# Two attention + FFN layers on one core: the prologue, the spreading of side steps, and the last chunk rearranged

## The chip, the cores and the metric

The kernel runs on one core of one Trainium2 chip. The metric is the device time of one execution in microseconds (us). The engines named below are TensorE (PE in the profile), VectorE (DVE), ScalarE (ACT), GpSimd (POOL), and SyncE (SP), which here only issues DMAs.

## The reference

Two identical layers work on x, 2048 tokens by 512 features in bf16. Cut to what matters:

```python
# H = 32 heads, Dh = 16, F = 1792
def A(x):                      # attention, on layernorm(x)
    q, k, v = split(x @ wqkv)                  # each (32, 2048, 16)
    p = softmax(q @ k.T * Dh ** -0.5)          # (32, 2048, 2048)
    return concat_heads(p @ v) @ wo
def B(x):                      # feed-forward, on layernorm(x)
    return silu(x @ w1) @ w2
for _ in range(2):
    x = x + A(layernorm(x))
    x = x + B(layernorm(x))
```

The layernorm has no weights; its eps is 1e-5.

## The kernel before, in words

Everything stays on the chip between the first load and the last store. x lies in SBUF as `x_sb`, 16 tiles of 128 tokens. The 2048 tokens are also cut into four **chunks** of 512, and the 32 heads into eight groups of four (`hb`; called "a head" in short). The order on TensorE, ScalarE and VectorE is the order in which the program is written (L541); GpSimd's and the DMAs' order is the framework's.

**The prologue.** For each chunk: statistics of four tiles (`ln_stats`, L147), a square root on ScalarE, then for each tile the normalisation on VectorE (`ln_apply`, L180), four transposes on TensorE and a VectorE copy into `xnT` (`transpose_tile`, L188). Then K of the first head group for all chunks (`k_two`), the maximum of |K| that makes a bound for the softmax (`amax_bm`), Q of the first head (`q_piece`) and V for all tokens (`v_two`, 64 matmuls).

**The loop of a layer** has 4 chunks of queries x 8 head groups x 16 key tiles = 512 **units** (L576). A unit is: two exponentials of 128 x 1024 scores on ScalarE (L585, `p_sb<-s_ps`), the four score matmuls of the next unit (L520), and four matmuls of p with V (L532, `o_ps`). V goes through `vd`, a block-diagonal copy that GpSimd fills every four units (L141). Scores pass through three PSUM tiles of two banks each (`spool`, the wide banks); `o_ps` has one bank, and all side work shares one other (`gpool`, the narrow one).

**Side steps.** All other matrix work of the layer runs inside the loop as *pieces*, lists of *steps* of mostly two matmuls: the transposes of a finished head (`heads_piece`), K and Q of the next head (`k_piece`, `q_piece`), and for the chunk before the output projection (`epilogue_pieces`), the feed-forward (`ffn_pieces`: layernorm, 14 pieces of w1 with a tanh on ScalarE, four y pieces of seven steps each), and the next layer's layernorm and V (`next_pieces`). A queue (the pump) decides how many steps run in each unit; work that the next head needs is put at its front. The number is a whole one:

```python
todo = -(-(total + later) // remaining) if total else 0
```

**The last chunk.** Its side work has no loop to hide in. After the last unit: heads, `epilogue_pieces` through the narrow bank, `ffn_last` (L467; the 512 tokens at once through the wide banks), in layer 0 also `next_pieces`, and then K for all chunks, the maximum and Q for the next layer's first head.

Of the kernel before, what the change touches and what calls it, by code (L numbers as in the profile page):

```python
# [18 lines left out]
def kernel(  # L19
# [34 lines left out]
    xnpool = ctx.enter_context(tc.tile_pool(name="xnpool", bufs=2))  # L54
# [25 lines left out]
    nc.gpsimd.memset(wk_pad[:], 0.0)  # L80
    nc.gpsimd.memset(wq_pad[:], 0.0)
# [3 lines left out]
    for j in range(4):  # L85
        nc.vector.memset(cw[0:1, 32 * j + 16 : 32 * j + 17], 1.0)
    E = cpool.tile([P, P], BF16, name="E")
# [4 lines left out]
    nc.vector.memset(eps_t[:], EPS)  # L92
    onescol = cpool.tile([P, 1], FP32, name="onescol")
# [6 lines left out]
    for c in range(NQC):  # L100
        nc.sync.dma_start(
            x_sb[:, 4 * c : 4 * c + 4, :],
            xf[512 * c : 512 * (c + 1), :].rearrange("(tt p) d -> p tt d", p=P),
        )
# [5 lines left out]
    nc.scalar.dma_start(wraw[:], A_wqkv[:, 0 : 2 * D].rearrange("(ct p) f -> p ct f", p=P))  # L110
    nc.scalar.dma_start(wv_sb[:], A_wqkv[:, 2 * D : 3 * D].rearrange("(ct p) f -> p ct f", p=P))
    for ct in range(CT):
        nc.gpsimd.tensor_copy(
            out=wk_pad[:, ct, :, 0:DH],
            in_=wraw[:, ct, D : 2 * D].rearrange("p (h d) -> p h d", d=DH),
        )
        nc.gpsimd.tensor_copy(
            out=wq_pad[:, ct, :, 0:DH],
            in_=wraw[:, ct, 0:D].rearrange("p (h d) -> p h d", d=DH),
        )  # L120
# [6 lines left out]
    amax = xpool.tile([P, HB], FP32, name="amax")  # L127
    vs = [vpool.tile([P, TT, D], BF16, name=f"v{i}", tag="v") for i in range(2)]
# [59 lines left out]
    def transpose_tile(xn, xnT, tq, wide_ps=False):  # L188
        if wide_ps:
            t_ps = spool.tile([P, CT, P], BF16, name="t4_ps", tag="s")  # L190
        else:
            t_ps = gpool.tile([P, CT, P], BF16, name="t_ps", tag="g")
        for ct in range(CT):
            nc.tensor.transpose(t_ps[:, ct, :], xn[:, ct * P : (ct + 1) * P], ident[:, :])  # L194
        nc.vector.tensor_copy(out=xnT[:, :, tq * P : (tq + 1) * P], in_=t_ps[:, :, :])


    def ln_steps(c, cell, act_sqrt=False, wide_ps=False):
# [7 lines left out]
        def rs():  # L206
            if act_sqrt:
                ln_rstd_act(cell["mvb"], cell["rstd"], 4)
            else:
                ln_rstd(cell["mvb"], cell["rstd"], 4)  # L210
            cell["xn0"] = ln_apply(cell["mvb"], cell["rstd"], 0, 4 * c)

        def tr(tq):
# [4 lines left out]
            transpose_tile(cell[f"xn{tq}"], cell["xnT"], tq, wide_ps)  # L218
# [30 lines left out]
    def k_two(xnTs, c, hb):  # L249
        k_ps = wide("k2_ps")  # L250
        for i in range(2):
            k_mm(xnTs[c + i], hb, k_ps[:, i, :], range(CT))
        nc.vector.tensor_scalar(
            out=KT[:, hb, c * 512 : (c + 2) * 512],
            in0=k_ps[:].rearrange("p a b -> p (a b)"),
            scalar1=onescol[:, 0:1], scalar2=None, op0=ALU.add,
        )

# [7 lines left out]
    def v_mm(xnT, tt, ps, cts):  # L266
        tq = tt % 4
        for ct in cts:
            nc.tensor.matmul(  # L269
                ps, lhsT=xnT[:, ct, tq * P : (tq + 1) * P], rhs=wv_sb[:, ct, :],  # L270
# [3 lines left out]
    def v_piece(cellx, tt, va):  # L274
        cell = {}

        def a():
            cell["ps"] = narrow("v_ps")
            v_mm(cellx["xnT"], tt, cell["ps"][:, :], (0, 1))

        def b():
            v_mm(cellx["xnT"], tt, cell["ps"][:, :], (2, 3))
            nc.vector.tensor_copy(out=va[:, tt, :], in_=cell["ps"][:, :])

        return [a, b]

    def v_two(xnT, tt, va):
        ps = wide("v2_ps")
        for i in range(2):
            v_mm(xnT, tt + i, ps[:, i, :], range(CT))  # L290
        nc.vector.tensor_copy(out=va[:, tt : tt + 2, :], in_=ps[:, :, :])
# [157 lines left out]
    def next_pieces(c, xnTs, va):  # L449
        cell = {}  # L450
        pieces = ln_steps(c, cell)
        for tq in range(4):
            pieces.append(v_piece(cell, 4 * c + tq, va))
# [13 lines left out]
    def ffn_last(c, emit_out):  # L467
        cell = {}
        run(ln_steps(c, cell, wide_ps=True))
        hT = htpool.tile([P, FT, 512], BF16, name="hT", tag="ht")  # L470
        for f2 in range(FT // 2):
            h_ps = wide("h2_ps")
            for i in range(2):
                h_mm(cell["xnT"], 2 * f2 + i, h_ps[:, i, :], range(CT))
            t_sb = tpool.tile([P, 2, 512], FP32, name="t_sb", tag="t")
            nc.scalar.activation(t_sb[:], h_ps[:], ACT.Tanh, scale=0.5)  # L476
            nc.vector.scalar_tensor_tensor(  # L477
                out=hT[:, 2 * f2 : 2 * f2 + 2, :], in0=t_sb[:], scalar=1.0, in1=h_ps[:],
                op0=ALU.add, op1=ALU.mult,
            )  # L480
        for tq in range(4):
            y_ps = spool.tile([P, 512], FP32, name="y3_ps", tag="s")
            y_mm(hT, tq, y_ps[:, :], range(FT))
            y_out(4 * c + tq, y_ps[:, :], emit_out)

    class Pump:
        def __init__(self):
            self.q = []

        def add(self, pieces):  # L490
            self.q += [list(p) for p in pieces]


        def front(self, pieces, begun):
            at = 1 if begun else 0
            self.q[at:at] = [list(p) for p in pieces]

        def steps(self):
            return sum(len(p) for p in self.q)

        def step(self):
            self.q[0].pop(0)()
            if not self.q[0]:
                self.q.pop(0)
# [179 lines left out]
```

## Time and profile before

| | us |
|---|---|
| runs (3), median | 2186.43 |
| runs, lowest to highest | 2184.53 to 2188.69 |
| profiled execution, time | 2192.17 |
| profiled execution, span | 2190.4 |
| TensorE busy in the span | 1952.9 (89%) |
| ScalarE busy | 1943.4 (89%) |
| VectorE busy | 558.6 (26%) |
| GpSimd busy | 248.2 (11%) |
| mean granted TensorE clock | 0.968 |

The span runs from the first instruction to the last. Times in the profile's rows are counted from the span's start. In a row of the timeline the first number is the start, the second the time in us, "x" the count of merged instructions, and the bracket the idle time of the engine just before and what ended it. In a row of a group, the last numbers are busy us, mean ns of one, and the idle time before. Instructions of one engine overlap in its pipeline, so the mean of one may be longer than the time from one start to the next.

### The profile page before, as it was taken

The numbers are of one execution on the slowest core, as the hardware profiler recorded it, in microseconds if no ns is written. First come the engines' busy times: TensorE is split into PE (matmuls) and PEld (weight loads), VectorE is DVE, ScalarE is ACT, GpSimd is POOL, SyncE is SP. The second block draws the span as 40 slices with busy tenths as digits, with TensorE's granted clock in tenths as the row PEclk, the third lists the DMA queues.
The fourth block names the chain that finished last, engine by engine and source line by source line (L and its number), as shares of the span: only waits on it lengthen the run. The fifth ranks groups of instructions, "written<-read, shape, count | busy, mean of one in ns | idle before, by whom it ended". The sixth has DMA issues, their size and how long they took to land.

```text
span 2190.4 us, 28490 instructions
## 1 busy us (share of the span) xinstructions
PE 1952.9 (89%) x10355; PEld 717.0 (33%) x10561; DVE 558.6 (26%) x1106; ACT 1943.4 (89%) x2152; POOL 248.2 (11%) x1055
## 2 busy tenths in 40 slices
PE   3999988999889998899778999998999989998996
PEld 1333323333333333333222333333333333333332
DVE  6323212112311133112343323131113111131114
ACT  0899989999799997999517999999999999999981
POOL 3111101111011110111000111111111111111100
PEclk9999999999899998999878999999999999999997
DMA  4000000000000000000000000000000000000000
GB/s 144 1 1 1 1 1 1 1 1 1 1 1 1 1 1 1 1 1 1 1 0 1 1 1 1 1 1 1 3 8 1 1 1 8 4 1 1 6 5 10
DMA packets 8477, 11.79 MB, mean 5 GB/s; under 512 B 400, under 2 KB 7312, under 8 KB 8336
## 3 DMA queue, kind: packets, MB, share of 16 engines
q1 hardware_dynamic: 7280, 8.39, 1.1%
q8 instruction: 82, 1.34, 0.3%
q10 hardware_dynamic: 1056, 1.57, 0.2%
q14 instruction: 59, 0.48, 0.1%
HBM read 7.86 MB, written 2.10 MB: 5 GB/s over the span
## 4 chain that ended last, share of the span: by engine, by line
PE 64%; ACT 21%; issue 8%; DVE 6%; DMA 0%; ACTq 0%; DVEq 0%
PE o_ps L532 30%; ACT p_sb L585 19%; PE s_ps L520 17%; PE y_ps L399 3%; PE k_ps L225 3%; PE q_ps L298 3%; PE h_ps L392 2%; PE y_ps L371 2%; PE v_ps L269 2%; ACT t_sb L429 1%; DVE st L149 1%; PE t_ps L194 1%; DVE oT L573 1%; PE at_ps L336 1%; DVE hT L477 1%
## 5 line engine op out<-in xcount | busy, mean ns | idle before, releaser
L585 ACT ACTIVATE p_sb<-s_ps 128x1024 bf16<-128x1024 f32 x2048 | 1920.4, 1237 | 123.3 <-PE s_ps L520 123.3
L532 PE MATMUL o_ps<-p_sb,vd 128*128 128x512 bf16 x3909 | 1045.1, 386 | 19.7 <-issue 15.5
L520 PE MATMUL s_ps<-QT,KT 17*128 17x512 bf16 x4096 | 575.3, 385 | 89.6 <-ACT p_sb L585 85.3
L532 PEld LDWEIGHTS <-vd 128*128 128x128 bf16 x4096 | 318.8, 98 | 484.8 <-issue 246.8
L141 POOL COPY vd<-v 128x64 bf16<-128x64 bf16 x1024 | 231.5, 239 | 1868.1 <-PE o_ps L532 1723.6
L520 PEld LDWEIGHTS <-KT 17*128 17x128 bf16 x4096 | 175.1, 91 | 591.1 <-issue 571.2
L573 DVE CAST oT<-o_ps 128x512 bf16<-128x512 f32 x64 | 44.3, 692 | 380.3 <-PE o_ps L532 380.3
L430 DVE SCALAR_TENSOR_TENSOR hT<-t_sb,h_ps 128x512 bf16<-128x512 f32 x84 | 57.5, 684 | 301.5 <-ACT t_sb L429 301.5
L399 PE MATMUL y_ps<-w_sb,hT 128*128 128x512 bf16 x445 | 128.0, 388 | 5.4 <-DVE hT L477 4.5
L392 PE MATMUL h_ps<-xnT,w_sb 128*128 128x512 bf16 x438 | 126.6, 387 | 3.2 <-DVE hT L477 1.4
L313 DVE CAST qc<-q_ps 128x512 bf16<-128x512 f32 x64 | 44.2, 691 | 173.0 <-PE q_ps L298 173.0
L242 DVE TENSOR_SCALAR KT<-k_ps,onescol 128x512 bf16<-128x512 f32 x56 | 42.0, 750 | 172.1 <-PE k_ps L225 172.1
L194 PE MATMUL t_ps<-ident,xn 128*128 128x128 bf16 x256 | 32.2, 271 | 57.1 <-DVE xn L182 55.4
L405 DVE SCALAR_TENSOR_TENSOR x_sb<-y_ps,x_sb 128x512 bf16<-128x512 f32 x32 | 22.1, 690 | 232.7 <-PE y_ps L399 232.7
L476 ACT ACTIVATE t_sb<-h_ps 128x1024 f32<-128x1024 f32 x14 | 14.3, 1024 | 75.1 <-PE h_ps L392 59.0
L298 PE MATMUL q_ps<-xnT,wq_pad 128*128 128x512 bf16 x255 | 77.0, 385 | 2.5 <-DVE attn L343 2.4
L225 PE MATMUL k_ps<-xnT,wk_pad 128*128 128x512 bf16 x254 | 78.7, 402 | 0.3 <-issue 0.2
L429 ACT ACTIVATE t_sb<-h_ps 128x512 f32<-128x512 f32 x84 | 76.9, 916 | 0.0
L399 PEld LDWEIGHTS <-hT 128*128 128x128 bf16 x448 | 44.3, 100 | 61.4 <-issue 6.1
L392 PEld LDWEIGHTS <-w_sb 128*128 128x128 bf16 x448 | 44.7, 100 | 58.4 <-issue 8.3
L327 DVE CAST QT<-q_ps 128x512 bf16<-128x512 f32 x64 | 44.2, 691 | 37.0 <-PE q_ps L322 37.0
L371 PE MATMUL y_ps<-wo_sb,aT 128*128 128x512 bf16 x126 | 40.8, 425 | 7.5 <-DVE aT L366 7.3
(58 smaller groups left out, 572.8 us busy)
## 6 DMA issues: line engine op xcount, KB each, us to landing
w_sb<-in_B_w_dram SPq DMA_DIRECT2D x2, 1792.0 KB, 15.0
x_sb<-in_A_x_dram SPq DMA_DIRECT2D x4, 512.0 KB, 9.8
out_dram<-x_sb SPq DMA_DIRECT2D x16, 128.0 KB, 1.7
wraw<-in_A_wqkv_dram ACTq DMA_DIRECT2D x1, 1024.0 KB, 7.6
wv_sb<-in_A_wqkv_dram ACTq DMA_DIRECT2D x1, 512.0 KB, 10.0
wo_sb<-in_A_wo_dram SPq DMA_DIRECT2D x1, 512.0 KB, 12.3
```

The source lines that it names most:

```text
L141: nc.gpsimd.tensor_copy(out=vdq[slot][:, :, j, 32 * j : 32 * j + DH], in_=va[:, NG * g : NG * (g + 1), DH * h : DH * (h + 1)],)
L225: nc.tensor.matmul(ps, lhsT=wk_pad[:, ct, 4 * hb : 4 * hb + 4, :].rearrange("p h s -> p (h s)"), rhs=xnT[:, ct, :], start=(ct == 0), stop= ...
L298: nc.tensor.matmul(cell["ps"][:, :], lhsT=wq_pad[:, ct, 4 * hb : 4 * hb + 4, :].rearrange("p h s -> p (h s)"), rhs=xnTs[c][:, ct, :], star ...
L371: nc.tensor.matmul(cell["ps"][:, :], lhsT=cell["aT"][:, ct, :], rhs=wo_sb[:, ct, :], start=(ct == 0), stop=(ct == CT - 1),)
L392: nc.tensor.matmul(ps, lhsT=w1_sb[:, ct, ft * P : (ft + 1) * P], rhs=xfT[:, ct, :], start=(ct == 0), stop=(ct == CT - 1),)
L399: nc.tensor.matmul(ps, lhsT=hT[:, ft, tq * P : (tq + 1) * P], rhs=w2_sb[:, ft, :], start=(ft == 0), stop=(ft == FT - 1),)
L429: nc.scalar.activation(t_sb[:, 0, :], hc["ps"][:, :], ACT.Tanh, scale=0.5)
L430: nc.vector.scalar_tensor_tensor(out=cell["hT"][:, ft, :], in0=t_sb[:, 0, :], scalar=1.0, in1=hc["ps"][:, :], op0=ALU.add, op1=ALU.mult,)
L520: nc.tensor.matmul(tiles[j // 2][:, j % 2, :], lhsT=KT[32 * j : 32 * j + VS, hb, kt * P : (kt + 1) * P], rhs=QT[32 * j : 32 * j + VS, :], ...
L532: nc.tensor.matmul(o_ps[:, :], lhsT=vdq[kt // NG % NR][:, kt % NG, j, :], rhs=p_sb[:, jj, :], start=(kt == 0 and j == 0), stop=(kt == TT - ...
L573: nc.vector.tensor_copy(out=oT[:], in_=o_ps[:])
L585: nc.scalar.activation(p_sb[:].rearrange("p a b -> p (a b)"), s_now[pr][:].rearrange("p a b -> p (a b)"), ACT.Exp, scale=float(SCALE),)
```

## The change

1. **Prologue.** The normalisation goes to ScalarE (`ln_apply_act`: Identity with scale rstd and bias -mean*rstd, `ln_nmr`), and so do the copies of the transposes of the first three chunks (`transpose_wide`). VectorE takes the statistics of a chunk and of the next one's first tile. K of the first head and the first 128 columns of V follow each chunk (`k_first_mm`, `v_first_mm`), with the maximum taken per chunk. The other 384 columns of V become steps of the first two heads. x is loaded in five DMAs, wk and wq in two, wk first; the memset of wk_pad moves from GpSimd to VectorE.
2. **Side steps.** Two queues, `must` and `side`; the rate is a fraction that is accumulated, no step runs in a head's first unit, and at unit 14 of a head `must` and the piece in hand are finished.
3. **Last chunk** (`last_chunk`). Transposes and projections go through the wide banks; statistics follow each tile; layernorm and feed-forward run in two halves of 256 tokens. For the next layer K of chunks 0 to 2 is computed in the loop (`k_first_piece`), so that only the last chunk's K, Q and V remain between the layers.

The diff, cut to its core:

```diff
-    xnpool = ctx.enter_context(tc.tile_pool(name="xnpool", bufs=2))
+    xnpool = ctx.enter_context(tc.tile_pool(name="xnpool", bufs=3))
-    nc.gpsimd.memset(wk_pad[:], 0.0)
+    nc.vector.memset(wk_pad[:], 0.0)
...
+    def ln_apply_act(nmr, rstd, i, tt):
+        xn = xnpool.tile([P, D], BF16, name="xn", tag="xn")
+        nc.scalar.activation(
+            xn[:], x_sb[:, tt, :], ACT.Identity, bias=nmr[:, i, :], scale=rstd[:, i, :]
+        )
+        return xn
+    def transpose_wide(src, dst, on_act):
+        t_ps = spool.tile([P, CT, P], BF16, name="t4_ps", tag="s")
+        for ct in range(CT):
+            nc.tensor.transpose(t_ps[:, ct, :], src[:, ct * P : (ct + 1) * P], ident[:, :])
+        if on_act:
+            nc.scalar.copy(dst, t_ps[:, :, :])
+        else:
+            nc.vector.tensor_copy(out=dst, in_=t_ps[:, :, :])
...
     for c in range(NQC):
-        cell = {}
-        run(ln_steps(c, cell, act_sqrt=True, wide_ps=True))
-        xnTs[c] = cell["xnT"]
+        cell = lns[c]
+        for i in range(1, 4):
+            ln_stats(cell["mvb"], i, 4 * c + i)
+        if c + 1 < NQC:
+            ln_stats(lns[c + 1]["mvb"], 0, 4 * c + 4)
+        ln_rstd_act(cell["mvb"], cell["rstd"], 4)
+        cell["nmr"] = ln_nmr(cell["mvb"], cell["rstd"], 4)
+        if k_prev is not None:
+            k_first_out(k_prev, c - 1)
+        xnTs[c] = xtpool.tile([P, CT, 512], BF16, name="xnT", tag="xt")
+        apply_transpose(cell, 4 * c, range(4), xnTs[c], c + 1 < NQC)
+        k_prev = k_first_mm(xnTs[c])
+        if c + 1 < NQC:
+            ps = v_first_mm(xnTs[c], c)
+            nc.scalar.copy(vs[0][:, 4 * c : 4 * c + 4, 0:P], ps[:, :, :])
+        if c == 1:
+            q_first[0]()
+            q_first[1]()
+    k_first_out(k_prev, NQC - 1)
+    amax_first()
+    q_first[2]()
...
         s_now = emit_s(QTs[0][0], 0, 0)
+        if L == 0:
+            ps = v_first_mm(xnTs[NQC - 1], NQC - 1)
+            nc.vector.tensor_copy(out=va[:, TT - 4 : TT, 0:P], in_=ps[:, :, :])
...
+                if L == 0 and c == 0 and hb < 2:
+                    for tt in range(8 * hb, 8 * hb + 8):
+                        add(must, [v_piece(lambda tt=tt: xnTs[tt // 4], tt, va, P, D)])
+                if c == NQC - 1 and hb == 1 and not last:
+                    add(side, [k_first_piece(nxt, k) for k in range(NQC - 1)])
...
-            total = pump.steps()
-            later = sum(3 for _ in range(hb + 1, HB)) + (HB - 1 - hb)
-            todo = -(-(total + later) // remaining) if total else 0
-            if left and kt < TT - 2 and pump.q:
-                todo = max(todo, 1)
-            pump_some(todo)
+            later = 4 * (HB - 1 - hb)
+            rate = (steps(must) + steps(side) + len(cur) + later) / remaining
+            if kt < TT - 2:
+                rate = max(rate, (steps(must) + len(cur)) / (TT - 2 - kt))
+            acc += rate
+            if kt == 0:
+                continue
+            while acc >= 1.0:
+                pump_one()
+                acc -= 1.0
             if kt == TT - 2:
-                tgt_c, tgt_hb = (c, hb + 1) if hb + 1 < HB else (c + 1, 0)
-                while tgt_c < NQC and QTs[tgt_c][tgt_hb] is None:
-                    pump_some(1)
+                while must or cur:
+                    pump_one()
```

The new last chunk, from `last_chunk` and the code behind it:

```python
for half in range(2):                    # projection, x and statistics, tile by tile
    for i in range(2):
        tq = 2 * half + i
        if tq < 3:
            heads_T(tq + 1)              # transposes to a wide bank, ScalarE copy
        # 4 matmuls with wo, x_sb += y_ps on VectorE, ln_stats
for half in range(2):
    ln_rstd(mvb, rstd, 2)                # then nmr, ScalarE apply, transposes, VectorE copy
    apply_transpose(cell, 4 * c, [2 * half, 2 * half + 1], xfT, False)
for half in range(2):
    for f0 in range(0, FT, 4):           # 4, 4, 4 and 2 w1 tiles of 256 tokens
        # 4 matmuls each, one tanh, one VectorE multiply into hT
for half in range(2):                    # y: 14 matmuls a tile, y_out; in layer 0 statistics
    ...
# between the layers:
for half in range(2):
    apply_transpose(mvs[half], 4 * c, [2 * half, 2 * half + 1], nxt[c], half == 0)
k_ps = k_first_mm(xnTs[c])
q_first[0]()
q_first[1]()
k_first_out(k_ps, c)
amax_first()
for tt in (4 * c, 4 * c + 2):
    v_two(xnTs[c], tt, vs[1])            # now copied by ScalarE
q_first[2]()
```

## The prediction, made before the changed kernel was run

> **What bounds the kernel now.** I read first the page's groups, then ScalarE's waits, its timeline, the two engines' unit of work in the timeline, and the busy time by stretch. The groups and waits (columns: busy us, mean ns | idle us before them):
>
> ```profile
> L585 ACT ACTIVATE p_sb<-s_ps 128x1024 bf16<-128x1024 f32 x2048 | 1920.4, 1237 | 123.3 <-PE s_ps L520 123.3
> L429 ACT ACTIVATE t_sb<-h_ps 128x512 f32<-128x512 f32 x84 | 76.9, 916 | 0.0
> ...
> ACT p_sb L585 <- PE s_ps L520: 123.3, 59, 45.2
> ACT t_sb L476 <- PE h_ps L392: 59.0, 2, 29.5
> ```
>
> ScalarE's exponentials fill 1920 of 2190 us; whatever is saved must be time in which they do not run. ScalarE's timeline says where that is:
>
> ```profile
> 65.23 34.99 ACT L585 ACTIVATE p_sb<-s_ps 128x1024 bf16<-128x1024 f32 x38 [28.91 <-PE s_ps L520]
> ...
> 308.47 1.94 ACT L585 ACTIVATE p_sb<-s_ps 128x1024 bf16<-128x1024 f32 x2 [1.25 <-PE s_ps L520]
> 313.75 1.94 ACT L585 ACTIVATE p_sb<-s_ps 128x1024 bf16<-128x1024 f32 x2 [3.35 <-PE s_ps L520]
> ...
> 968.21 103.16 ACT L585 ACTIVATE p_sb<-s_ps 128x1024 bf16<-128x1024 f32 x112
> 1100.85 1.02 ACT L476 ACTIVATE t_sb<-h_ps 128x1024 f32<-128x1024 f32 x1 [29.49 <-PE h_ps L392]
> ...
> 1161.29 5.61 ACT L585 ACTIVATE p_sb<-s_ps 128x1024 bf16<-128x1024 f32 x6 [45.19 <-PE s_ps L520]
> ```
>
> So: 65.2 us until the first exponential; 1071.4 to 1161.3 between the layers, 89.9; from 2129.6 (last exponential's end) to 2190.4 behind them, 60.8. Inside the loops ScalarE waits 2.8 us in layer 0's first chunk, 39.4 in its other three, almost all in the 37 us after each chunk's start (305 to 345 and its two repeats), and 7.1 in all of layer 1.
>
> How near TensorE stands to ScalarE inside the loop, a unit (one key tile) at a time:
>
> ```profile
> 200.94 0.50 PE L520 MATMUL s_ps<-QT,KT 17*128 17x512 bf16 x4
> 201.37 1.04 PE L532 MATMUL o_ps<-p_sb,vd 128*128 128x512 bf16 x4
> 202.25 0.59 PE L225 MATMUL k_ps<-xnT,wk_pad 128*128 128x512 bf16 x2
> 202.77 0.50 PE L520 MATMUL s_ps<-QT,KT 17*128 17x512 bf16 x4
> 203.21 1.04 PE L532 MATMUL o_ps<-p_sb,vd 128*128 128x512 bf16 x4
> 204.17 0.39 PE L520 MATMUL s_ps<-QT,KT 17*128 17x512 bf16 x2
> ```
>
> A unit with one side step of two matmuls takes 202.77 - 200.94 = 1.83, one without 1.40. ScalarE's two exponentials take 1.84 (32 in 29.44). One step per unit is exactly what fits; a second one in the same unit is late by 0.43, and more if it must wait for VectorE. TensorE's lead is worth some 0.8: it stands 0.79 for oT at every head and ScalarE loses 0.16.
>
> Why a chunk's start costs 13 us: the pump runs two steps a unit there, and two waits in a row are followed by matmuls at 0.43 each (308.3 to 311; "cold" below) instead of 0.22 (four from 201.37 to 202.25):
>
> ```profile
> 306.23 0.40 PE L336 MATMUL at_ps<-ident,oT 128*128 128x128 bf16 x4 [0.79 <-DVE oT L573]
> 307.44 0.61 PE L298 MATMUL q_ps<-xnT,wq_pad 128*128 128x512 bf16 x2 [0.81 <-DVE attn L343]
> 308.31 2.26 PE L532 MATMUL o_ps<-p_sb,vd 128*128 128x512 bf16 x6
> ...
> 305.00:345.00 40.00, 31.72 (x168) 11.86 (x170) 15.59 (x42) 26.98 (x29) 3.15 (x14) 0.83 0.00 1
> ```
>
> The last row is the stretch's busy time by engine; its 0.83 is the granted clock, 1.00 in the stretches beside it.
>
> **1. Prologue, +16.5.** Before: four serial blocks of VectorE work (stats, apply, copy), then K, Q and 64 V matmuls, first exponential at 65.2. After, the built order on ScalarE is, per chunk: Sqrt, apply 0, apply 1, copy 0, apply 2, copy 1, apply 3, copies 2 and 3, and then the copy of 16 V matmuls (128 columns each) that stand behind the chunk's 4 K matmuls. That copy is the added wait: the next chunk's Sqrt is queued behind it. A 128x512 copy or Identity of ScalarE isn't in the trace; it lies between 0.48 (a 128x512 tanh to the next exponential) and 1.02 (128x1024 alone). I take 0.55, near the row of its size. One chunk: Sqrt to first apply 0.74 (0.54 before, and one 128x4 operation of 0.20), eight operations 4.4, waits for transposes 0.3, K 4 x 0.43, V 16 x 0.11, copy and latencies 0.8: 9.7. The first Sqrt comes at 10.2 as before (five tiles of stats at 0.80 behind a first tile near 6). Three chunks reach 39.3; the last has four applies and VectorE copies (4.1), K 1.75, KT 0.85, a quarter of the 2.29 reduction, Bm and the small reduction 0.5, q's last matmul 0.6, QT 0.75, scores 0.3: 48.7. Saved 16.5. With K and V at 0.22 it is 5 us more, at 0.75 per ScalarE operation 6 less: 10 to 22. The wk_pad memset on VectorE (about 1.8 by its 128x1 and 128x128 memsets, 3.5 on GpSimd) lies in VectorE's 5.28 us wait for x. The extra DMA issues cost 0.5 each on idle queues. The wk copies, first on GpSimd now, end near 11, K wants them at 16.
>
> The rows behind this price: before, K at 39.1 went at 0.43 each behind transposes and waits, and V from 49.2 at 0.25. [...]
>
> **2. V moved into the first two heads, -15.5.** The other 384 columns, 64 matmuls of 0.16, become steps of heads 0 and 1 of the first chunk: 28 and 29 steps in 14 units. The built order of TensorE, units priced as 1.40 + matmuls + waits, against 1.84:
> Head 0: 8 K matmuls and 2 extra PV in one unit, with one wait for KT (0.75 row, 0.85): 4.4, over by 2.5; two units of 4 K 0.8; q's second half and its Bm matmul in one unit, waiting 1.1 for qc and qu: 3.14, over by 1.3; eight units of four V matmuls 0.2 each, 1.6; the 16 V matmuls between the first two score groups 0.6. Sum 6.8.
> Head 1: heads' transposes and 6 K in one unit, waits 0.81 and 0.85: over by 2.8; 6 K with a wait 1.7; 4 K 0.4; q 1.3; V 1.6; less the lead 0.8: 7.0.
> The first units run cold behind the prologue: 14 matmuls at 0.43 add 3.0. Heads 2 to 6 join the transposes with a K step: 1.40 + 0.3 + 0.81 + 0.43, over by 1.1, less 0.8, 0.3 each: 1.5. Together 18.3 against 2.8. If the K waits hide it is 10, if the clock falls in head 1 too it is 24.
>
> **3. Chunks 1 to 3 of layer 0, +28.** The rate is now 109 steps plus 28 foreseen in 128 units: 1.07, not 2. The build gives one step per unit, a double about once a head. What remains: the transposes joined with q once or twice a chunk (0.3), and y pieces of 7 steps that are flushed at a head's unit 14: 14 matmuls in one unit are 3.0, over by 2.55, less 0.8 = 1.75. From the order: chunk 1: one full flush, two triples 1.0, joined 0.6: 3.3; chunk 2: 14 and 12 matmuls, 3.5; chunk 3: 12 and 14 in one head, 4.5. Sum 11.3 against 39.4. Bounds: 6 (lead larger) to 19 (a burst also delays the next step).
>
> **4. Layer 1's loop, -1.** It had one step a unit already. Twelve joined steps (0.3), two flushes of 12 and 14 matmuls in chunk 2 (3.0), triples in chunks 1 and 3 (1.6): about 8 against 7.1. Bounds +3 to -6.
>
> **5. Between the layers, +24.** From the last exponential, attn is ready at 2.6 as before. Then transposes go to wide banks with ScalarE's copies; VectorE bounds: add and stats 1.55 x 4 from 4.85 to 11.1 (19.8 before, when they ran in turn with transposes). Two half rstd of 2.4 each with nmr, apply and transposes between: h starts at 20.5, before at 25.8. First tanh 24.0 against 29.5. t_sb still has one buffer, so tanh and multiply alternate at 2.37; six such and two half groups of 1.4 end at 41. y no longer waits for the last of them: it starts when a bank comes free at 37.2, 4 x 3.0 to 49.2 where before it ended at 57.4; 1.7 more if its first eight are cold as they were. Next layer's LN: half 0 under y; half 1 ends 12.5 behind y's second tile (43.2, half a cold start 0.9): xnT at 56.6 against 68.6. Then only one chunk's K (4) and q (4) cold 3.5, V (16) 3.4 to 5, which stands ahead of the Bm matmul, 0.4, QT 0.75, scores 0.3: 9.1, where 16 V, 16 K, a 2.29 reduction and a serial q took 21.3. First exponential at 65.7 against 89.9. Bounds 17 to 29.
>
> **6. Tail, +7.** Same steps to y's end: 8.2, less half a cold start. Bounds 3 to 10.
>
> Sum 16.5 - 15.5 + 28 - 1 + 24 + 7 = 59.0. The profiled execution took 2192.17 (span 2190.4): 2133.2. The median of the runs, 2186.43, is 5.7 lower: 2127.4.
>
> **Rivals.**
> Bursts eat the spread (16%): part 3 keeps only 10 and part 2 costs 22, as the bursts and joined steps bring back the clock drop of 305 to 345. For: the flushes are in the order. Against: they are dense matmuls, not waits. 59 - 18 - 6.5: 2152.
> The prologue and the gaps run better (10%): K and V warm, banks free earlier: +6, +5, +3, part 2 at 10: +5: 2108.
> The other side (4%): the joined transposes. 23 units let q or K wait 0.81 right behind the transposes. Where that happened at 307 the next three units lost 1.25 + 3.35 + 1.71 = 6.3. If each did, 23 x 6.3 = 145 against 59: 2213, slower. It decides from 2.6 each. Against: there two waits came in a row; with oT a unit earlier only one is left, and at the 0.79 alone of every head the clock stayed at 1.00.
> That part 1 doesn't do what it says (ScalarE at 1.02 an operation) costs 13 more: 2140, inside the range.
>
> **How the numbers follow.** 70% for the sum. The terms' half-widths, 6, 7, 6.5, 4.5, 6 and 3.5, give 14 in quadrature; those on the clock move together, so 20. With the first two rivals the range is 2105 to 2152. Slower takes the third rival's 4%; within 0.2% (4 us, about what a measurement of this kernel tells from none) 1%.
>
> **What would show it.** Right: first exponential near 49; ScalarE's waits of 15 to 20 in the first chunk, near 11 in the next three with none over 2.5; 66 between the layers; 54 at the end. Wrong: a granted clock under 0.95 in 110 to 1050, first exponential past 55, or ScalarE waiting over 1 us at most heads.

## The result, and the profile after

The changed kernel takes 2244.91 us (median of 4 runs, 2243.56 to 2245.89), beside it the kernel before 2187.56 (4 runs, the three above and one more, 2184.53 to 2189.0): a ratio of 1.0264, 95% interval 1.0246 to 1.0281. It is 57 us slower where 59 us of gain were forecast, and far outside the range of 2105 to 2152. The profiled execution after has a span of 2242.2 (2190.4 before): 51.8 more.

The exponentials' group and the tanh group on the page of the changed kernel (columns: busy us, mean ns | idle us before them), and then ScalarE's waits:

```profile
L703 ACT ACTIVATE p_sb<-s_ps 128x1024 bf16<-128x1024 f32 x2048 | 1904.5, 1171 | 90.1 <-PE s_ps L617 88.1
L489 ACT ACTIVATE t_sb<-h_ps 128x512 f32<-128x512 f32 x84 | 58.2, 693 | 52.1 <-PE h_ps L452 49.7
```
```profile
ACT p_sb L703 <- PE s_ps L617: 88.1, 68, 5.9
ACT t_sb L489 <- PE h_ps L452: 49.7, 40, 1.4
```

Before, the same tanh group had an idle time of 0.0. That is the new thing on this page: in the loop ScalarE now waits before tanh, 52.1 us in all (49.7 of it put down to h_ps), while the number of tanh and of exponentials is the same.

ScalarE's timeline of the changed kernel shows the three regions outside the loops, and a head's length in layer 1:

```profile
55.60 1.94 ACT L703 ACTIVATE p_sb<-s_ps 128x1024 bf16<-128x1024 f32 x2 [5.91 <-PE s_ps L617]
...
1046.20 53.37 ACT L703 ACTIVATE p_sb<-s_ps 128x1024 bf16<-128x1024 f32 x58 [1.16 <-PE s_ps L617]
...
1164.38 5.61 ACT L703 ACTIVATE p_sb<-s_ps 128x1024 bf16<-128x1024 f32 x6 [0.38 <-PE s_ps L617]
...
1203.32 29.44 ACT L703 ACTIVATE p_sb<-s_ps 128x1024 bf16<-128x1024 f32 x32 [1.16 <-PE s_ps L617]
1233.91 29.44 ACT L703 ACTIVATE p_sb<-s_ps 128x1024 bf16<-128x1024 f32 x32 [1.16 <-PE s_ps L617]
```

The first exponential is at 55.6 (65.2 before), between the layers pass 1164.38 - 1099.57 = 64.8 (89.9), the tail is 53.2 (60.8). So the three regions outside the loops all became shorter. But heads are now separated by 1.16 of idle ScalarE in places where before it was 0.16, and the loops are longer: layer 0 from first to last exponential 1044.0 (1006.1), layer 1 1024.7 (968.3). Summed in ScalarE's idle time against before:

| part | forecast, gain | measured, gain |
|---|---|---|
| 1 first exponential | +16.5 | +9.6 (55.6 against 65.2) |
| 2 first chunk of layer 0 | -15.5 | -16.4 (19.2 against 2.8) |
| 3 its other three chunks | +28 | -17.4 (56.8 against 39.4) |
| 4 layer 1's loop | -1 | -52.8 (59.8 against 7.0) |
| 5 between the layers | +24 | +25.1 |
| 6 tail | +7 | +7.6 |
| the loops grew by 37.9 and 56.4; what of it is in no wait (not taken apart) | none | -7.7 |
| sum | +59.0 | -52.0 (span -51.8) |

Parts 3 and 4 hold 97 of the 111 us between forecast and result. Where a tanh waits, the rows of TensorE and ScalarE in the changed kernel read like this (here and below the other engines' rows are left out):

```profile
1467.89 0.50 PE L617 MATMUL s_ps<-QT,KT 17*128 17x512 bf16 x4
1468.32 1.04 PE L629 MATMUL o_ps<-p_sb,vd 128*128 128x512 bf16 x4
1469.20 0.59 PE L452 MATMUL h_ps<-xnT,w_sb 128*128 128x512 bf16 x2
1469.72 0.39 PE L617 MATMUL s_ps<-QT,KT 17*128 17x512 bf16 x2
1469.83 0.60 ACT L489 ACTIVATE t_sb<-h_ps 128x512 f32<-128x512 f32 x1 [0.96 <-PE h_ps L452]
1470.32 5.60 ACT L703 ACTIVATE p_sb<-s_ps 128x1024 bf16<-128x1024 f32 x6
1471.39 0.39 PE L617 MATMUL s_ps<-QT,KT 17*128 17x512 bf16 x2 [1.28 <-ACT p_sb L703]
```

The w1 matmuls end at 1469.79 and the tanh starts at 1469.83: the program put both into one unit, behind that unit's exponentials, so ScalarE came to the tanh 0.96 before its input existed. The next unit's scores had been done since 1468.39 (the first row's end), before ScalarE fell idle at 1468.87; but the program puts the tanh ahead of their exponentials, and ScalarE keeps that order. Then TensorE in turn waits 1.28 for a bank of scores. In the kernel before the tanh came a unit later than its matmuls:

```profile
1455.82 0.59 PE L392 MATMUL h_ps<-xnT,w_sb 128*128 128x512 bf16 x2
1456.35 0.50 PE L520 MATMUL s_ps<-QT,KT 17*128 17x512 bf16 x4
...
1456.96 0.85 ACT L429 ACTIVATE t_sb<-h_ps 128x512 f32<-128x512 f32 x1
```

Its input had been done since 1456.41, and there is no wait.

Counted unit by unit, 42 of the 84 tanh steps of the changed kernel share a unit with their matmuls. Units of a head are counted from 0: 21 are at unit 14, where the piece in hand is finished whatever it is; 16 at unit 1, because the rate accumulated over the skipped first unit makes unit 1 take two steps; 5 at unit 13. These 42 are the ones that wait, 52.0 us in all.

The other cost is at the heads, here a boundary in layer 0's first chunk of the changed kernel:

```profile
133.33 0.39 PE L617 MATMUL s_ps<-QT,KT 17*128 17x512 bf16 x2 [0.53 <-ACT p_sb L703]
133.65 1.47 PE L629 MATMUL o_ps<-p_sb,vd 128*128 128x512 bf16 x6
134.96 0.39 PE L396 MATMUL at_ps<-ident,oT 128*128 128x128 bf16 x4
136.16 0.61 PE L255 MATMUL k_ps<-xnT,wk_pad 128*128 128x512 bf16 x2 [0.81 <-DVE attn L403]
136.69 0.40 PE L617 MATMUL s_ps<-QT,KT 17*128 17x512 bf16 x4
137.18 5.67 ACT L703 ACTIVATE p_sb<-s_ps 128x1024 bf16<-128x1024 f32 x6 [1.15 <-PE s_ps L617]
```

The transposes do not wait for oT any more, as forecast. But the K step joined to them waits 0.81 for attn and stands ahead of the next scores: from the second half of one unit's scores to the next scores 136.69 - 133.33 = 3.36 against ScalarE's 1.84, and ScalarE loses 1.15.

### The profile page after: what moved, and what is told of

It is laid out like the page before. It is cut to its first block, busy times and chain, and to the rows that moved or that the text cites. A ratio compares the mean times of both kernels' runs of the same rounds, so it can differ in the third digit from the quotient of the medians.

```text
span 2242.2 us, 28818 instructions
## 1 busy us (share of the span) xinstructions
PE 1974.8 (88%) x10531; PEld 735.6 (33%) x10737; DVE 549.0 (24%) x1122; ACT 1987.4 (89%) x2209; POOL 244.5 (11%) x1054
## 4 chain that ended last, share of the span: by engine, by line
PE 66%; ACT 22%; issue 6%; DVE 4%; ACTq 0%; another core or an unknown queue 0%; DVEq 0%
PE o_ps L629 31%; ACT p_sb L703 19%; PE s_ps L617 19%; PE y_ps L459 4%; PE h_ps L452 3%; PE q_ps L358 3%; PE k_ps L255 2%; ACT t_sb L489 2%; PE v_ps L322 1%; PE y_ps L431 1%; PE at_ps L396 1%; PE q_ps L382 1%; DVE hT L575 1%; DVE attn L403 0%; ACT t_sb L574 0%
## 5 line engine op out<-in xcount | busy, mean ns | idle before, releaser
L617 PE MATMUL s_ps<-QT,KT 17*128 17x512 bf16 x4096 | 611.9, 384 | 144.3 <-ACT p_sb L703 136.6
L459 PE MATMUL y_ps<-w_sb,hT 128*128 128x512 bf16 x436 | 113.7, 379 | 3.1 <-DVE hT L575 2.7
L489 ACT ACTIVATE t_sb<-h_ps 128x512 f32<-128x512 f32 x84 | 58.2, 693 | 52.1 <-PE h_ps L452 49.7
L452 PE MATMUL h_ps<-xnT,w_sb 128*128 128x512 bf16 x326 | 95.3, 379 | 1.1 <-DVE QT L387 0.8
L207 PE MATMUL t_ps<-ident,xn 128*128 128x128 bf16 x112 | 15.8, 292 | 48.9 <-ACT xn L198 48.0
L452 PEld LDWEIGHTS <-w_sb 128*128 128x128 bf16 x336 | 32.9, 98 | 40.6 <-issue 1.1
L402 DVE RECIPROCAL rec<-at_ps 128x16 f32<-128x16 bf16 x64 | 16.4, 257 | 117.9 <-PE at_ps L396 117.9
L150 DVE BATCH_NORM_STATS2 st<-x_sb 128x6 f32<-128x512 bf16 x64 | 43.2, 674 | 3.6 <-DMA x_sb<-in_A_x_dram 3.2
```

The source lines that it names most:

```text
L452: nc.tensor.matmul(ps, lhsT=w1_sb[:, ct, ft * P : (ft + 1) * P], rhs=xfT[:, ct, :], start=(ct == 0), stop=(ct == CT - 1),)
L459: nc.tensor.matmul(ps, lhsT=hT[:, ft, tq * P : (tq + 1) * P], rhs=w2_sb[:, ft, :], start=(ft == 0), stop=(ft == FT - 1),)
L489: nc.scalar.activation(t_sb[:, 0, :], hc["ps"][:, :], ACT.Tanh, scale=0.5)
L617: nc.tensor.matmul(tiles[j // 2][:, j % 2, :], lhsT=KT[32 * j : 32 * j + VS, hb, kt * P : (kt + 1) * P], rhs=QT[32 * j : 32 * j + VS, :], ...
```

## The experiments

Theory A, formed from these lines: ScalarE's waits at joined steps (a tanh in the unit of its matmuls; a K or q step behind a head's transposes) are the loss. The rivals: the granted clock falls at the joined transposes (the prediction's third rival); the y bursts of up to 14 matmuls at unit 14; the fractional rate itself. The clock rival loses at once: the mean granted clock is 0.975 after and 0.968 before, so the slower kernel had the higher one, and in the stretch from 110 to 1050, for which the prediction named its sign, it is 0.99 (0.98 before). In the experiments it lies between 0.971 and 0.980, but for e10 with 0.962.

e1 to e8, e10 and e11 are one run each, e1 to e8 beside a kernel before of 2188.2, e9 to e11 beside 2186.7 (median of 9). Gains and losses below are against the changed kernel's 2244.9 unless said otherwise. "Waits" are ScalarE's in the loops, "the next three" are chunks 1 to 3 of layer 0.

**e1_first_unit: the change, but steps run in a head's first unit again.**

```diff
-            if kt == 0:
-                continue
             while acc >= 1.0:
```

> The changed kernel, but steps may run in a head's first unit again. Theory A (steps that wait on another engine stand in the wrong unit: the skip of the first unit puts the head's transposes into the second one, which holds six PV matmuls, and pushes two steps into one unit, so that 16 of the 42 tanh that share a unit with their own matmuls arise there): head stalls of 1.15 us fall to 0.16 at some 27 heads, 16 x 1.3 of tanh waits go: 45 to 48 us less, about 2198. Theory B (the flush at unit 14 is the cost): hardly less, 2240. Theory C (transposes joined with a following step drop the clock): 23 joined places become 1, so also less, but with the granted clock rising from 0.975; under A the clock stays.

Measured 2199.82. Counted unit by unit, the joined transposes fall from 23 to 1 and the joined tanh from 42 to 26; the waits are 16.4 in the first chunk, 27.4 + 16.9 (14 tanh) in the next three, 19.5 + 11.5 (12 tanh) in layer 1. The skipped first unit alone costs 45 us, as theory A had it (2198): it moves nothing away, it makes the second unit take two steps.

**e2_no_side_flush: at unit 14 only what the next head needs is finished.**

```diff
-                while must or cur:
+                while must or (cur and hand["must"]):     # hand: the piece in hand came from must
```

> The changed kernel, but at unit 14 only pieces that the next head needs are finished, not the side piece in hand. Theory A: tanh sharing a unit with their matmuls fall from 42 to 20 (22 x 1.2 = 27 us) and the seven bursts of 12 or 14 y matmuls go (10 us), joined transposes rise from 23 to 27 (+4): about 2212. Theory B: all of the loops' loss of some 78 us goes, 2167. Theory C: no change or slower (more joined places), 2245 to 2250.

Measured 2199.53. Joined tanh fall from 42 to 20, and ScalarE's waits before tanh follow, from 52.0 to 21.0. The y bursts fall from 7 to 0 at the same time, and the waits for scores in the loops from 83.8 to 70.6. Theory A had expected less (2212), as it let the four more joined transposes cost 4 and the bursts 10. This run does not tell tanh and bursts apart by itself; the trace of the changed kernel does. Here is one of its bursts:

```profile
481.92 3.18 PE L459 MATMUL y_ps<-w_sb,hT 128*128 128x512 bf16 x14
...
485.53 5.61 ACT L703 ACTIVATE p_sb<-s_ps 128x1024 bf16<-128x1024 f32 x6 [2.10 <-PE s_ps L617]
```

ScalarE waits 1.7 to 2.4 behind each of the seven, 13.7 in all, where the forecast had 1.75 each. So the bursts cost something, and about what was forecast.

**e3_tanh_alone: a tanh step never shares a unit; bursts and the skipped unit stay.**

```diff
+            d.alone = True                # d: the tanh step
             pieces.append([a, b, d])
...
+            ran = 0
             while acc >= 1.0:
+                if ran and cur and getattr(cur[0], "alone", False):
+                    break
+                alone = bool(cur) and getattr(cur[0], "alone", False)
                 pump_one()
+                ran += 1
                 acc -= 1.0
+                if alone:
+                    break
...
-                while must or cur:
+                while must or (cur and (not (len(cur) <= 2 and getattr(cur[-1], "alone", False)))):
```

> The changed kernel, but a tanh step never shares a unit with another step. Theory A: all 42 tanh waits (52 us) go, but the steps move up and 39 instead of 23 units join the head's transposes with a following step (16 x 1.0) and 11 instead of 7 y bursts remain (+6): about 2215. Theory B: unchanged or slower, 2245 to 2255. Theory C: slower by the 16 more joined places, 2290.

Measured 2214.1, as expected. Not one tanh waits any more (52.0 us in the changed kernel), but only 31 us come back: the rule pushes steps to the heads, joined transposes rise from 23 to 39, the bursts from 7 to 11, and the waits for scores rise to 47.0 in chunks 1 to 3 and 39.2 in layer 1. The two costs are fed from the same place: steps that are held back in one unit join in another.

**e4_old_pump: the integer rule of before, with prologue, V steps and last chunk as changed.**

```diff
-            rate = (steps(must) + steps(side) + len(cur) + later) / remaining
-            if kt < TT - 2:
-                rate = max(rate, (steps(must) + len(cur)) / (TT - 2 - kt))
-            acc += rate
-            if kt == 0:
-                continue
-            while acc >= 1.0:
+            total = steps(must) + steps(side) + len(cur)
+            todo = -(-(total + later) // remaining) if total else 0
+            if (must or cur) and kt < TT - 2:
+                todo = max(todo, 1)
+            if L == 0 and c == 0 and hb < 2 and kt < TT - 1:
+                todo = max(todo, -(-steps(must) // (TT - 1 - kt)))
+            for _ in range(todo):
                 pump_one()
-                acc -= 1.0
             if kt == TT - 2:
-                while must or cur:
+                while must or (cur and hand["must"]):
```

> The changed kernel with the number of steps per unit by the rule of before (a whole number, steps in the first unit, no flush of side pieces); prologue, V as steps of the first two heads, and last chunk stay changed. All theories that put the loss into the spreading: before's 2187.6, less 9.6 at the prologue, 25 between the layers, 7.6 at the tail, plus 16 in the first two heads: 2162. If the loss came from what the other parts leave behind (clock, ScalarE's extra work), it stays above 2200.

Measured 2175.75: faster than before by 12, and 69 faster than the change. So the loss against before sits in how steps are dealt out. The run missed its number by 14: the waits are 18.7 in the first chunk, 39.7 + 2.3 in the next three and 8.5 in layer 1, where the last two groups are those of before, and the layer 0 loop is 22.6 longer; that takes more than half of what prologue (+9.6), gap (+23.6) and tail (+7.6) gain.

**e5_heads_alone: the change, with nothing behind a head's transposes in their unit.**

```diff
+        a.alone = True                    # a: a head's transposes
         return [a]
...
             while acc >= 1.0:
+                nxt_step = cur[0] if cur else (must or side or [[None]])[0][0]
                 pump_one()
                 acc -= 1.0
+                if getattr(nxt_step, "alone", False):
+                    break
```

> The changed kernel (first unit still skipped, flush as it is), but nothing runs behind a head's transposes in their unit. Theory A (the joined unit is priced 1.83 + 0.3 + 0.81 + 0.43 because the second unit of a head holds six PV matmuls, so ScalarE loses 1.15): the 27 gaps of 1.1 to 1.2 us fall to 0.2 or none, the tanh waits stay: some 25 us less, about 2219. Rival (it is the skip of the first unit itself, not the joining): gaps stay, 2240.

Measured 2219.41, 25.5 less, as theory A had it. ScalarE's gaps of 1.05 to 1.25 before an exponential fall from 25 to 7; the tanh waits stay (28.1 and 24.9). So both costs are in the change, each by itself: here the heads' is gone and the tanh's stays, in e3 the other way round.

**e6_rules: the fractional rate, with five rules.** Steps run in the first unit; at unit 14 only what the next head needs is finished; a second step in a unit only from the same piece, at most two; tanh and q's last step alone; at most one step is carried over.

```diff
+        d.alone = True                    # in q_piece and ffn_pieces, d: q's last step, the tanh step
...
-            if kt == 0:
-                continue
-            while acc >= 1.0:
+            ran = 0
+            while acc >= 1.0 and ran < 2:
+                q = must if must else side
+                step = cur[0] if cur else (q[0][0] if q else None)
+                if ran and (not cur or getattr(step, "alone", False)):
+                    break
                 pump_one()
                 acc -= 1.0
+                if not getattr(step, "free", False):     # free: the small Bm step
+                    ran += 1
+                if getattr(step, "alone", False):
+                    break
+            acc = min(acc, 1.0)
             if kt == TT - 2:
-                while must or cur:
+                while must or (cur and hand["must"]):
```

> The changed kernel with the fractional rate kept, but with rules on what may share a unit: steps in the first unit, only needed pieces finished at unit 14, a second step only from the same piece, tanh and q's last step alone. Theory A (spreading evenly pays what was forecast, 11 us of stalls in chunks 1 to 3 and 8 in layer 1, once no step shares a unit with a wait): tanh waits none, head gaps 0.2, first two heads 9 instead of 19: 2245 - 10 - 53 - 56 = 2126 to 2132. Rival D (one step a unit is already too tight for TensorE, so ScalarE waits wherever the steps go): no better than the old rule, 2170 or more.

Measured 2136.87, 5 over the range of theory A and 33 under rival D. A head of layer 0 now reads as before:

```profile
493.23 29.44 ACT L707 ACTIVATE p_sb<-s_ps 128x1024 bf16<-128x1024 f32 x32 [0.16 <-PE s_ps L621]
522.83 29.44 ACT L707 ACTIVATE p_sb<-s_ps 128x1024 bf16<-128x1024 f32 x32 [0.16 <-PE s_ps L621]
```

The waits are 8.3 in the first chunk, 8.7 in the next three, 12.1 in layer 1, none before tanh. The forecast left 11.3 and 8 of waits in parts 3 and 4, 19.3; with these rules, which the change does not have, they are 20.8. The rival that the fractional rate is the cause falls with it, as the formula of the rate is the change's own. The bursts are gone too under these rules, so this run says nothing of them.

**e7_rules_q_later: e6, with the prologue's q moved behind the third chunk's statistics.**

```diff
     for c in range(NQC):
...
+        if c == 2:                        # behind k_first_out
+            q_first[1]()
...
         if c == 1:
             q_first[0]()
-            q_first[1]()
```

> The same, and the second half of the first head's q (two matmuls, then qc and qu on VectorE) comes behind the third chunk's statistics instead of ahead of them. If the missing 3.8 us of the prologue is VectorE's queue (qc waits for q's matmuls from 22.6 to 31.0 with the third chunk's statistics behind it), the first exponential comes 3 to 4 us earlier (52 instead of 55.6) and the time falls by the same. If ScalarE's own chain sets it, nothing changes.

Measured 2134.44 and 51.93 for the first exponential (55.62 in e6_rules). The 3.7 at the first exponential are as expected. The time is 2.4 less; single runs of this kernel differ by up to 3.5 (e9), so the time alone would not show it. What it takes away is this, in the changed kernel:

```profile
29.87 1.10 PE L358 MATMUL q_ps<-xnT,wq_pad 128*128 128x512 bf16 x4
31.02 0.69 DVE L373 CAST qc<-q_ps 128x512 bf16<-128x512 f32 x1 [8.44 <-PE q_ps L358]
31.95 0.69 DVE L150 BATCH_NORM_STATS2 st<-x_sb 128x6 f32<-128x512 bf16 x1
...
34.48 0.30 ACT L155 ACTIVATE std<-mvb,eps_t 128x4 f32<-128x4 f32 x1 [3.77 <-DVE mvb L151]
```

VectorE waits 8.44 for q's matmuls with the third chunk's statistics queued behind that wait, and so ScalarE's Sqrt of that chunk waits 3.77. In e7 the Sqrt comes at 30.84 and has no wait:

```profile
30.84 0.30 ACT L155 ACTIVATE std<-mvb,eps_t 128x4 f32<-128x4 f32 x1
```

**e8_V_in_prologue: e7, with all of V computed in the prologue and no V steps in the first two heads.**

```diff
-        ps = spool.tile([P, 4, P], FP32, name="v0_ps", tag="s")
-        for tq in range(4):
-            v_mm(xnT, 4 * c + tq, ps[:, tq, :], range(CT), 0, P)
-        return ps
+        for tq in (0, 2):
+            v_two(xnT, 4 * c + tq, vs[0])
...
-                if L == 0 and c == 0 and hb < 2:
-                    for tt in range(8 * hb, 8 * hb + 8):
-                        add(must, [v_piece(lambda tt=tt: xnTs[tt // 4], tt, va, P, D)])
```

> The same as the kernel before it in this call, but all of V is computed in the prologue, none as steps of the first two heads. If V's move pays (forecast: it costs the loop 13 us more than nothing, and the prologue is the worse place, since its matmuls run at 0.43): first exponential 15 to 20 us later, first chunk's stalls 7 us less, 10 to 17 us slower. If the move was a loss: up to 5 us faster.

Measured 2146.91, 12.5 slower than e7; the first exponential is at 69.66 instead of 51.93, and the 17.7 lost there buy only 1.8 of the first chunk's 6.6 of waits (4.8 here). Against this form of the prologue, part 2 of the change, which the forecast priced at a loss of 15.5, pays with the rules of e6. It is not the form of the kernel before: V's eight copies are of 128x1024 and on ScalarE here (1.01 each), ahead of the first exponential, where before VectorE made them. And V's matmuls do not run at 0.43, as was expected: in the second chunk the second copy, eight matmuls behind the first, starts 1.73 after it (35.76 against 34.03, both behind a wait for v_ps), 0.22 each. How much of the 17.7 is matmuls and how much is ScalarE's order was not taken apart.

**e10_all_tanh_joined: the best kernel (that of e7, timed again in e9), with all 84 tanh in the unit of their matmuls.**

```diff
-            d.alone = True
+            d.behind = True               # d: the tanh step
...
                 pump_one()
                 acc -= 1.0
+                while cur and getattr(cur[0], "behind", False):
+                    pump_one()
+                    acc -= 1.0
```

> The same kernel, but every tanh step runs in the unit of its own matmuls: 84 of them instead of none. Nothing is added to any engine, TensorE's order hardly changes. Theory A: each costs ScalarE what it cost in the changed kernel, 52.0 us / 42 = 1.24, so 84 x 1.24 = 104 and 2238; ScalarE's waits for h_ps near 100 on the page. Rival (a unit is priced by TensorE alone, as the prediction did): a tanh costs TensorE nothing, so 2134, within 5.

Measured 2250.18, 116 slower than the same kernel without it (2133.92) and 12 over theory A's figure. ScalarE's waits in e10, and then its wait for scores in e9_best:

```profile
ACT t_sb L490 <- PE h_ps L453: 96.2, 84, 2.4
ACT p_sb L708 <- PE s_ps L621: 47.1, 70, 5.9
```
```profile
ACT p_sb L708 <- PE s_ps L621: 33.5, 60, 5.9
```

All 84 wait, 1.15 each; the waits for scores rise from 33.5 to 47.1, which is most of the rest of the 116. The granted clock is lower here, 0.962 against 0.980; that may be a part of the rest, but the 96.2 stand before the tanh alone. TensorE has the same matmuls to do: a unit priced by TensorE alone shows nothing of this.

**e11_heads_joined: the best kernel, with one more step behind every head's transposes.**

```diff
+        a.more = True                     # a: a head's transposes
         return [a]
...
                 pump_one()
                 acc -= 1.0
+                if getattr(step, "more", False):
+                    pump_one()
+                    acc -= 1.0
+                    break
```

> The same kernel as e9_best, but every head's transposes take the next step (a K or q step) into their unit, the first of a head, which holds two PV matmuls: some 62 joined units. Theory A (it is the transposes in the second unit, with six PV, that make a joined unit cost 1.15): in the first unit, two score groups' start 0.36, two PV 0.52, oT 0.79, transposes 0.39, attn 0.81, two matmuls 0.5 are 3.4 against 1.84 with a lead of 0.8, so 0.7 each and 62 x 0.7 = 43: 2177. The prediction's price of 0.3 each: 2153. Rival (joining itself costs 1.15 wherever it stands): 2205. No cost: 2134.

Measured 2203.23: 69 slower, not 43, and within 2 of the rival's 2205. The waits for scores rise from 33.5 to 102.2, and 68.7 / 62 boundaries (31 in each layer) = 1.11 each. The row of the waits, and a joined unit in this kernel:

```profile
ACT p_sb L709 <- PE s_ps L622: 102.2, 98, 5.9
```
```profile
121.13 0.66 PE L622 MATMUL s_ps<-QT,KT 17*128 17x512 bf16 x4
121.72 0.60 PE L634 MATMUL o_ps<-p_sb,vd 128*128 128x512 bf16 x2
...
123.11 0.40 PE L397 MATMUL at_ps<-ident,oT 128*128 128x128 bf16 x4 [0.79 <-DVE oT L699]
...
124.32 0.60 PE L255 MATMUL k_ps<-xnT,wk_pad 128*128 128x512 bf16 x2 [0.81 <-DVE attn L404]
124.86 0.40 PE L622 MATMUL s_ps<-QT,KT 17*128 17x512 bf16 x4
...
125.35 2.86 ACT L709 ACTIVATE p_sb<-s_ps 128x1024 bf16<-128x1024 f32 x3 [1.26 <-PE s_ps L622]
```

I had put the 1.15 of the changed kernel down to the second unit's six PV matmuls. That part of theory A falls: in the first unit, with two PV, the joined step costs as much, because the wait of 0.79 for oT stands where the four further PV (0.87) were. It is the joining that costs, in either unit.

**e9_best: e7 once more, timed for an interval.**

> The kernel of e7_rules_q_later again, timed against the kernel before in five rounds for an interval. Theory A (ScalarE's waits at joined steps were the whole difference between sum and result, and the change's other parts are worth what was measured): 2134.4 again, a ratio of 0.975 to 0.977 to the kernel before.

Measured 2133.92 (5 runs, 2131.67 to 2135.19) beside 2186.73: a ratio of 0.9762, interval 0.9748 to 0.9776. It beats both kernels, and its profiled span of 2129.8 (before 2190.4) can be read by the forecast's own parts: first exponential 52.0 (+13.2), first chunk 6.9 (-4.1), the next three 8.7 (+30.7), layer 1's loop 12.2 (-5.2), between the layers from 1033.87 to 1101.12, 67.3 (+22.6), tail 53.8 (+7.0). These add up to 64.2; the spans differ by 60.6, and the 3.6 between are in no wait.

## Why the prediction was wrong

**Parts 3 and 4: the failed step.** The prediction priced a unit by TensorE alone ("the build gives one step per unit, a double about once a head"), with the doubles that it saw in the order at 0.3 each and the flushes by their matmuls. Two things were missing.

First, a step that runs on ScalarE was given no price. The order on TensorE doesn't show it, as a tanh is no matmul; the order on ScalarE does: a tanh directly behind the exponentials of the unit that issues its matmuls. 42 of them cost 1.24 each, 52.0 us, and e10 puts it at 84 for 96.2. The flushes at unit 14 were counted for y, where they are dense matmuls; 21 of the 42 joined tanh come from the same flush.

Second, the lead of 0.8 was misread. The prediction took it from a head's boundary, where TensorE "stands 0.79 for oT at every head and ScalarE loses 0.16". The same boundary in the trace of before, whole:

```profile
1432.25 0.50 PE L520 MATMUL s_ps<-QT,KT 17*128 17x512 bf16 x4
1432.68 0.60 PE L532 MATMUL o_ps<-p_sb,vd 128*128 128x512 bf16 x2
...
1434.07 0.40 PE L336 MATMUL at_ps<-ident,oT 128*128 128x128 bf16 x4 [0.79 <-DVE oT L573]
1434.40 0.39 PE L520 MATMUL s_ps<-QT,KT 17*128 17x512 bf16 x4
```

That unit holds two PV matmuls instead of four. From scores to scores it is 2.15, only 0.31 over ScalarE's 1.84, and ScalarE loses 0.16 of that: the lead is worth 0.15 here, not 0.8. A joined unit of 2.94 then costs 0.95, not 0.3. The trace after has a unit of 3.36, longer by the second unit's two further PV matmuls, and a loss of 1.15.

The waits for scores in parts 3 and 4 are 29.7 and 34.8 where 11.3 and 8 were forecast, 45 more; with the 52.0 of tanh these are the 97 of the table. Each wait can be put down to the unit whose steps stand just ahead of the awaited scores. The joined transposes, 17 of the 23 in these parts, then hold 25.2: 14 of them 1.15 each and three 2.7 to 3.5, where 0.3 each, 5, were priced. The seven bursts hold 13.7 where 12 were priced, so there the sum was right. The remaining 25.6 stand behind other units, such as those with q's last step or a double, for which some 2 were priced; no run takes these apart. That joined heads cost 1.1 each is shown by e11, and that both parts come to the forecast's size under rules that leave no joined step and no burst, by e6.

**The third rival** was right on the side and, at 20 of the 23 units, wrong on the way: joined transposes do lose more than 0.3, but there the granted clock was 1.00 (from 3.0 ahead of the joined step's start to 1.0 behind it), and 19 of the 20 lost their 1.15 or 1.16 by ScalarE's plain wait (the other 3.02, with four more K matmuls and a wait of 0.84 for KT). At the other three, those of 2.7 to 3.5, the clock was 0.50 to 0.52, but it had fallen ahead of the transposes: to 0.69 from 316 to 318, 0.57 from 1576 to 1578 and 0.63 from 2098 to 2100, where the transposes start at 318.13, 1580.89 and 2100.02. Nor did the kernel before have the clock at 1.00 at every 0.79 wait for oT: of the 63 heads' transposes from 66 to 2130, 27 had that wait, 25 of them at 1.00 (from 0.8 ahead of the transposes to 2.0 behind their start) and two at 0.81 and 0.77. Its point of decision, 2.6 at each of 23, was not reached: they lost 34.0 in all, 1.5 each on average. Its time was also summed wrongly: 145 lost against 59 gained leaves 86 over the 2186 of before, some 2272, not 2213.

**Part 1** was mis-sized, 9.6 for 16.5. The Sqrt of chunks 1, 2 and 3 came at 20.4, 34.5 and 44.7 where 19.9, 29.6 and 39.3 were worked out, and the first exponential 10.9 behind the last where 9.4 was: 0.5, 4.4, 0.5 and 1.5 late. Most of it lies in the 4.4 and is a queue that the prediction had followed on ScalarE and not on VectorE: qc waits for q's matmuls with the next chunk's statistics behind it (shown by e7: 3.7 at the first exponential). The rest, some 3.2, was not tested; ScalarE's applies start 0.71 apart where 0.55 was taken. K was priced cold, at 0.43 a matmul, and is no faster:

```profile
16.35 1.87 PE L255 MATMUL k_ps<-xnT,wk_pad 128*128 128x512 bf16 x4 [0.67 <-ACT xnT L209]
```

Four K matmuls in 1.87 are 0.47 each, against 0.22 in the loop.

**Part 2** met its number, 19.2 against 18.3, in part by luck. It was priced with units, waits and a lead as in parts 3 and 4, but its heads have no tanh. Head 0 lost 7.3 where 6.8 and 3.0 for a cold start were priced (the granted clock was 0.50 from 55.6 to 59 and 0.63 from 59 to 66), and head 1 lost 6.1 for 7.0. Heads 2 to 6, joined as in parts 3 and 4, lost 1.15 each, 5.8 where 1.5 was priced. The error of the joined step is there too, and the other terms made up for it. e6 shows that more than half of it was the dealing too (8.3 with the rules).

**Parts 5 and 6** held: 64.8 against 65.7 and 53.2 against 53.8. They are chains without a queue that deals steps out, worked row by row, and part 5 held on its way as well: counted from the last exponential, w1 starts at 20.4 (20.5 forecast), the first tanh at 23.5 (24.0), y ends at 48.9 (49.2) and xnT is done at 55.8 (56.6).

## What to carry to other kernels

When steps are dealt into the units of a loop, price each unit on every engine that works in order, not on the bound of TensorE alone: a step that consumes what the same unit produces can stop the other engine for the whole way from its own work to that result, although no engine has more to do (1.15 for each of 84 tanh in e10). Before using a lead as cover for many events, measure it in a unit whose content is the usual one: a wait of 0.79 that costs 0.16 says nothing of 0.63 to spare when the same unit lacks two matmuls. And a rate that is evened out over units gains only if the rules say which steps may stand together: the same fractional rate gave 2245 without such rules and 2137 with them (e6).

## What the runs showed of the chip beside that

A ScalarE apply (Identity with a scale and bias per partition, 128x512 bf16 from SBUF to SBUF) starts every 0.71 in the changed kernel (four in 2.93, the last of them 0.81 long), slower than its 128x512 copies of transposes out of PSUM, of which two follow one another at 0.49 (1.07 for both, 0.58 for one). And moving work out of the prologue into the loop can pay although TensorE is busy 90% of the loop (850 of the 940 us from 110 to 1050 in the changed kernel): with the 384 columns of V and their copies on ScalarE in the prologue (e8) the first exponential came 17.7 later, and in the loop (e7) the same matmuls cost 1.8 of waits (12.5 in the whole time, one run each).
